# Twelve disjoint views for indirect stores, and a conversion split two issues on, in an attention + expert + feed-forward kernel

## Chip, cores, metric

One core of a Trainium2 chip runs the whole program. The metric is device microseconds of one execution. PE is TensorE, DVE is VectorE, ACT is ScalarE, POOL is GpSimd, SP is SyncE; the last issues most of the loads.

## What is computed

Three layers follow each other on 1536 tokens of width 512, in float32. The first is chunked attention with memory keys. The second sends each token to one of eight experts. The third is a plain feed-forward network. Cut to what matters here:

```python
def _moe_ref(x, w_gate, w1, w2, capacity):
    expert_idx = np.argmax(x @ w_gate, axis=1)
    ...
    h = np.maximum(np.einsum('ecd,edf->ecf', disp, w1), 0.0)
    y = np.einsum('ecf,efd->ecd', h, w2)
    ...
            out[i] = gate_w[i] * y[expert_idx[i], pos[i]]

def _moe2_ref(x, w_in, w_out):
    h = x @ w_in
    g = np.maximum(0.01 * h, h)
    return (g @ w_out)
```

## The kernel before, in words

**Stages.** `prologue` does attention and routing. `experts` then runs expert 0 to 7 one after the other (`expert`, line 746), and `ffn` (line 918) does the last layer. Every float32 product is made of three products of high and low parts, so each weight is first converted into such a pair by ACT and DVE.

**Expert stage.** For each expert, POOL gathers rows of x from HBM by an index table (`gather`, line 634, `nat` tiles, five buffers; line 636 is the indirect DMA). PE transposes them (line 730, in `expert_x`) during the phases of the expert before, then multiplies (line 767, and line 774 for the second product). An expert with over 256 tokens first runs `block` for the rest. The gathers of expert e+2 are issued in phase 3 of expert e (`gathers(e + 2)`). In expert 1, phases 2 and 3 also work out the order in which tokens are sorted by expert (`order`, `sort`): `sort` makes twelve indirect stores of 128 records of three words into the HBM tensor `table` (line 683), and then loads the sorted table back as `srt` (line 685). All of these are in POOL's one queue, in program order, so the gathers of expert 4, issued in expert 2, stand behind the twelve stores and the load.

**Feed-forward stage.** `ffn` makes 48 steps: four quarters of the hidden width (q), three groups of 512 tokens (g), four slices (f). Step n does `gemm3` (line 937, 12 matmuls), `act_h` (ACT lines 943 and 945, DVE lines 944 and 946), then `gemm4` of step n-2 (line 957, 12 matmuls). When a group's four slices are done, `add_up` adds the sums to the output tile, by DVE (line 971) from the second quarter on, and in the last quarter POOL stores each of the twelve tiles of 128 rows to its sorted place by an indirect store (line 973).

**Conversion pieces of the feed-forward weights.** `weights_gen` hands out the 32 pieces of this stage one by one; each `feed(1)` issues one. A piece goes through three parts: at its own issue ACT squares and scales it (lines 128 and 129); one issue later DVE does six operations on it (lines 131 to 139, "the six" below); and `FLIGHT` issues after its own it is split into high (ACT, line 117) and low part (DVE, line 118). Only then it counts as ready. `need` forces an extra `feed` when a product wants a piece that is not ready yet. When no weight slot is free, a feed advances the pieces in flight and issues none. The feeds of the feed-forward stage are given by `FEED_FFN`, nine per quarter for eight pieces:

```python
FEED_FFN = (0, 2, 3, 4, 6, 7, 8, 10, 11)
...
                if rec[1] == 1 or rec[1] == rec[2]:
                    next(rec[0], None)
```

**Order.** Each engine runs its instructions in program order. Waits are put in by a tracker of tile and tensor accesses. It takes two indirect stores into the same tensor for a possible overlap, because the rows are known only at run time.

Of the kernel before, what the change touches and what calls it, by code (L numbers as in the profile page):

```python
# [1 line left out]

# [3 lines left out]

F32 = mybir.dt.float32
# [12 lines left out]
B, H, S, D = 2, 8, 768, 64  # L20
# [7 lines left out]
TPB = S // P  # L28
# [2 lines left out]
RING = 8  # L31
NQ = 4
RAWS, MORE = 5, 3
FLIGHT = 3
SHARE = (0,)
GAP_FEED = 2
WARM = (6, 8, 28)
# [12 lines left out]
class Builder:  # L50
# [470 lines left out]
    def prologue(self):  # L521
        nc = self.nc
        with ExitStack() as ctx:
# [53 lines left out]
            self.wgen = self.weights_gen()  # L577
            self.flight, self.share, self.quarter = FLIGHT, SHARE, 0
            for u in range(NU + 4):
# [99 lines left out]
        dv.tensor_tensor(out=self.rec[:, :, 1], in0=last, in1=keep, op=ALU.mult)  # L679

    def sort(self):
        for t in range(B * TPB):
            self.nc.gpsimd.indirect_dma_start(out=self.table, out_offset=bass.IndirectOffsetOnAxis(
                ap=self.place[:, t:t + 1], axis=0), in_=self.rec[:, t, :], in_offset=None)
        self.nc.gpsimd.dma_start(out=self.srt, in_=self.table.rearrange("(t p) c -> p t c", p=P))

# [231 lines left out]
    def ffn(self):  # L918
        nc = self.nc
        NG, GT, HQ = 3, 512, 4  # L920

        for kind in "AB":
            self.weight_slot((kind, E, 1))
        self.X.append(self.slot(("X", 2), [P, 2, KD, GT], F32R, "x2"))
        wide = self.slot("O", [P, 8, DM], F32, "total")
        rest = [self.mp.tile([P, 2, DM], F32, name="rest", tag="xs", bufs=4) for _ in range(2)]
        total = [wide[:, t, :] for t in range(8)] + [rest[t // 2][:, t % 2, :] for t in range(4)]
        X, nat = self.X, self.rows_of(2, self.ys)
        hps, gs, acc = {}, {}, {}

        def gemm3(s):
            q, g, f = s
            w = self.weight("A", E, q * HQ + f)
            c = slice(f * P, f * P + P)
            hps[s] = self.mps.tile([P, GT], F32, name="h", tag="h", bufs=3)
            for n, (wi, xi, k) in enumerate((wi, xi, k) for wi, xi in ((1, 0), (0, 0), (0, 1)) for k in range(KD)):
                nc.tensor.matmul(hps[s], w[:, wi, k, c], X[g][:, xi, k, :], start=(n == 0), stop=(n == 11))  # L937

        def act_h(s):
            hp = hps.pop(s)  # L940
            t = self.mp.tile([P, GT], F32, name="t", tag="o", bufs=2)
            gt = gs[s] = self.mp.tile([P, 2, GT], F32R, name="gt", tag="hg", bufs=4)
            nc.scalar.copy(out=t, in_=hp)  # L943
            nc.vector.scalar_tensor_tensor(out=t, in0=hp, scalar=0.01, in1=t, op0=ALU.mult, op1=ALU.max)  # L944
            nc.scalar.copy(out=gt[:, 0, :], in_=t)  # L945
            nc.vector.tensor_tensor(out=gt[:, 1, :], in0=t, in1=gt[:, 0, :].bitcast(F32), op=ALU.subtract)  # L946

        def gemm4(ss):
            q, g, f = ss[-1]
            ws = {s: self.weight("B", E, q * HQ + s[2]) for s in ss}  # L950
            gt = {s: gs.pop(s) for s in ss}
            if ss[0][2] == 0:
                acc[g] = [self.mps.tile([P, DM], F32, name="acc", tag="acc", bufs=4) for _ in range(4)]
            for i in range(4):
                for s in ss:
                    for n, (hi, wi) in enumerate(((0, 1), (0, 0), (1, 0))):
                        nc.tensor.matmul(acc[g][i], gt[s][:, hi, i * P:(i + 1) * P], ws[s][:, wi, s[2], :],  # L957
                                         start=(s[2] == 0 and n == 0), stop=(s[2] == HQ - 1 and n == 2))
            if f == HQ - 1:
                add_up(q, g, acc.pop(g))  # L960
                if g == NG - 1:
                    self.retired |= {("A", E, q), ("B", E, q)}

        def add_up(q, g, parts):
            for i in range(4):
                t = g * 4 + i
                sc, o = self.srt[:, t, 2:3].bitcast(F32), total[t]
                if q == 0:
                    nc.scalar.activation(out=o, in_=parts[i], func=AF.Copy, scale=sc)
                else:  # L970
                    nc.vector.scalar_tensor_tensor(out=o, in0=parts[i], scalar=sc, in1=o, op0=ALU.mult, op1=ALU.add)  # L971
                if q == NQ - 1:
                    nc.gpsimd.indirect_dma_start(out=self.out, out_offset=bass.IndirectOffsetOnAxis(  # L973
                        ap=self.srt[:, t, 0:1], axis=0), in_=o, in_offset=None)

        steps = [(q, g, f) for q in range(NQ) for g in range(NG) for f in range(HQ)]
        for n, s in enumerate(steps):
            q, g, f = s
            gemm3(s)
            act_h(s)  # L980
            if 1 < n < len(steps) - 2:
                gemm4([steps[n - 2]])
            if q == 0 and g == 1:
                self.make_x(2, f, nat)
            self.quarter = q + 1
            self.feed(n % len(steps[::NQ]) in FEED_FFN)
        gemm4(steps[-4:-3])
        gemm4(steps[-3:-2])
        gemm4(steps[-2:])
# [61 lines left out]
```

## Time and profile before

| what | value |
|---|---|
| runs before (three) | 617.01, 619.18, 621.42 us; median 619.18 |
| profiled execution | 616.79 us, its span 615.0 us |
| granted TensorE clock, mean | 0.94 |
| packets of the DMA queues | 66377, 84.83 MB |

The span runs from the first to the last instruction that the profiler recorded; the 1.79 us beside it lie outside. Three kinds of views are used below. A timeline row gives start in us, duration in us, engine, line, operation, output<-input, shapes and count; in brackets stands how long the engine sat idle before and what released it. A row of waits gives the sum of idle us, how often, and the longest. A row of windows gives busy time of each engine in a stretch, the granted clock, the share of the DMA engines and GB/s.

### The profile page before, as it was taken

To read this page: it belongs to the slowest core of one execution; us is meant where nothing else is said; L and a number is where in the kernel's file an instruction comes from. 1 tells how busy PE (TensorE), PEld (TensorE's weight loads), DVE (VectorE), ACT (ScalarE), POOL (GpSimd) and SP (SyncE) were. 2 spreads that over 40 slices of the span, in tenths; PEclk is the share of its full clock that TensorE was granted. 3 is DMA by queue.
4 is the path that set the end of the run, shared out by engine and by line. 5 is a ranking of instruction groups with operands and counts; after the bars stand their busy time and mean duration, and the time that the engine had idled before them with its cause. 6 is when DMAs were issued, how large, how long until landed. Compare 5 with 4: busy or idle time off the path is not lost.

```text
span 615.0 us, 9309 instructions
## 1 busy us (share of the span) xinstructions
PE 536.1 (87%) x3313; PEld 433.1 (70%) x3313; DVE 408.6 (66%) x686; ACT 299.9 (49%) x520; POOL 97.8 (16%) x132
## 2 busy tenths in 40 slices
PE   7899948998979594998979999999999999999980
PEld 5566636886967482777967778878877887878870
DVE  5777776864471238882797877868888788854430
ACT  7999646752451348762544455453443444332110
POOL 7422243031211313103102000000000000001121
PEclk7999977998999696899999999999999999999995
DMA  8989949969448529974244212212222110000011
GB/s 190 202 207 193 284 147 352 386 202 305 121 101 227 144 90 341 358 238 155 103 138 137 69 68 70 68 36 68 69 68 70 46 58 0 1 0 35 38 66 68
DMA packets 66377, 84.83 MB, mean 138 GB/s; under 512 B 23168, under 2 KB 39568, under 8 KB 66320
## 3 DMA queue, kind: packets, MB, share of 16 engines
q1 hardware_dynamic: 60016, 66.46, 36.7%
q0 software_dynamic: 5296, 15.77, 8.2%
q10 hardware_dynamic: 1008, 1.84, 0.8%
q8 instruction: 37, 0.61, 0.4%
q14 instruction: 20, 0.16, 0.1%
HBM read 70.66 MB, written 13.39 MB: 137 GB/s over the span
## 4 chain that ended last, share of the span: by engine, by line
DVE 29%; PE 16%; ACT 5%; issue 4%; DMA 2%; ACTq 0%; POOLq 0%
PE acc L957 7%; PE h L937 6%; DVE t L944 4%; DVE gt L946 3%; ACT gt L945 3%; DVE c L138 3%; DVE c L135 3%; DVE c L131 3%; DVE ring L118 3%; DVE c L133 2%; DVE c L137 2%; DVE total L971 2%; DVE c L139 1%; DMA out_dram<-rest,srt 1%; DVE x L697 1%
## 5 line engine op out<-in xcount | busy, mean ns | idle before, releaser
L957 PE MATMUL acc<-ring,gt 128*128 128x512 f32 x576 | 139.1, 391 | 7.7 <-DVE rest L971 2.9
L937 PE MATMUL h<-x,ring 128*128 128x512 f32 x576 | 140.7, 394 | 4.7 <-DVE ring L118 3.7
L957 PEld LDWEIGHTS acc<-ring,gt 128*128 128x128 f32 x576 | 107.5, 188 | 33.4 <-ACT t L943 6.4
L937 PEld LDWEIGHTS h<-x,ring 128*128 128x128 f32 x576 | 108.8, 190 | 28.1 <-DVE ring L118 4.1
L945 ACT CAST gt<-t 128x512 fp32r<-128x512 f32 x48 | 29.8, 621 | 93.7 <-DVE t L944 93.7
L946 DVE TENSOR_TENSOR gt<-t,gt 128x512 fp32r<-128x512 f32 x48 | 33.3, 693 | 33.0 <-ACT gt L945 32.3
L225 DVE TENSOR_TENSOR ring<-raw,ring 128x1024 fp32r<-128x1024 f32 x43 | 50.3, 1221 | 3.1 <-ACT ring L221 2.7
L944 DVE SCALAR_TENSOR_TENSOR t<-h,t 128x512 f32<-128x512 f32 x48 | 32.9, 685 | 29.0 <-ACT t L943 29.0
L767 PE MATMUL h<-xsT,ring 128*128 128x256 f32 x384 | 50.9, 292 | 0.6 <-ACT ring L221 0.6
L943 ACT COPY t<-h 128x512 f32<-128x512 f32 x48 | 28.0, 583 | 46.0 <-PE h L937 45.9
L767 PEld LDWEIGHTS h<-xsT,ring 128*128 128x128 f32 x384 | 49.2, 200 | 1.3 <-ACT ring L221 1.0
L973 POOL DMA_INDIRECT out_dram<-total,srt x8 | 7.8, 975 | 258.9 <-DVE total L971 241.7
L819 DVE SCALAR_TENSOR_TENSOR hs<-h,hs 128x512 fp32r<-128x512 f32 x32 | 21.7, 687 | 41.1 <-ACT hs L818 41.1
L774 PE MATMUL acc<-ring,hs 128*128 128x512 f32 x192 | 45.6, 392 | 0.0
L221 ACT CAST ring<-raw 128x1024 fp32r<-128x1024 f32 x43 | 42.5, 1059 | 0.0
L774 PEld LDWEIGHTS acc<-ring,hs 128*128 128x128 f32 x192 | 35.4, 188 | 6.9
L128 ACT ACTIVATE c<-raw 128x512 f32<-128x512 f32 x32 | 21.9, 684 | 24.8 <-DVE ring L118 24.8
L636 POOL DMA_INDIRECT nat<-xs,tab x24 | 25.3, 1054 | 53.6 <-PE tp L730 36.4
L818 ACT ACTIVATE hs<-h 128x512 fp32r<-128x512 f32 x32 | 18.9, 605 | 26.9 <-PE acc L774 26.9
L867 PE MATMUL h<-ring,xc 128*128 128x512 f32 x72 | 21.6, 452 | 7.9 <-ACT xc L853 7.8
L730 PE MATMUL tp<-ident,nat 128*128 128x128 f32 x64 | 12.9, 329 | 14.5 <-DMA nat<-xs,tab 10.6
L779 PE MATMUL h<-ring,xsT 128*128 128x512 f32 x72 | 22.7, 476 | 3.1 <-DMA nat<-xs,tab 1.5
(183 smaller groups left out, 805.9 us busy)
## 6 DMA issues: line engine op xcount, KB each, us to landing
raw<-in_moe_w_dram SPq DMA_DIRECT2D x43, 512.0 KB
more<-in_moe_w_dram SPq DMA_DIRECT2D x21, 512.0 KB
raw<-in_moe_w_in_dram SPq DMA_DIRECT2D x16, 512.0 KB
raw<-in_moe_w_out_dram SPq DMA_DIRECT2D x16, 512.0 KB
kn<-in_k_dram SPq DMA_DIRECT2D x16, 192.0 KB
qn<-in_q_dram SPq DMA_DIRECT2D x16, 192.0 KB
xs<-x POOLq DMA_DIRECT2D x16, 192.0 KB, 4.7
ys<-o SPq DMA_DIRECT2D x12, 256.0 KB
```

The costliest lines, as they stand in the source:

```text
L221: self.nc.scalar.copy(out=hi, in_=raw)
L225: eng.tensor_tensor(out=lo[:, j:j + n], in0=raw[:, j:j + n], in1=hi[:, j:j + n].bitcast(F32), op=ALU.subtract)
L636: self.nc.gpsimd.indirect_dma_start(out=t, out_offset=None, in_=src, in_offset=bass.IndirectOffsetOnAxis(ap=idx[:, col:col + 1], axis=0))
L767: nc.tensor.matmul(hps[f // 2][:, f % 2 * 256:f % 2 * 256 + 256], w["A", f // 4][:, wi, k, c], xs[xi][:, k, :], start=(n == 0), stop=(n == ...
L774: nc.tensor.matmul(y[j], hs[f // 2][:, hi, c:c + P], w["B", f // 4][:, wi, f % 4, :], start=(f == 0 and n == 0), stop=(f == 7 and n == 2))
L779: nc.tensor.matmul(hps[i], xs[xi][:, k, :P], w["A", i][:, wi, k, :], start=(n == 0), stop=(n == 11))
L937: nc.tensor.matmul(hps[s], w[:, wi, k, c], X[g][:, xi, k, :], start=(n == 0), stop=(n == 11))
L943: nc.scalar.copy(out=t, in_=hp)
L944: nc.vector.scalar_tensor_tensor(out=t, in0=hp, scalar=0.01, in1=t, op0=ALU.mult, op1=ALU.max)
L945: nc.scalar.copy(out=gt[:, 0, :], in_=t)
L946: nc.vector.tensor_tensor(out=gt[:, 1, :], in0=t, in1=gt[:, 0, :].bitcast(F32), op=ALU.subtract)
L957: nc.tensor.matmul(acc[g][i], gt[s][:, hi, i * P:(i + 1) * P], ws[s][:, wi, s[2], :], start=(s[2] == 0 and n == 0), stop=(s[2] == HQ - 1 a ...
```

## The change

`sort` and `ffn` each ask for twelve views of their tensor that the tracker takes as disjoint, and each of the twelve indirect stores goes through its own view. The addresses and the data are the same. `FLIGHT` goes from 3 to 2, so that a piece is split one issue earlier.

```diff
+from concourse.ap import dram_disjoint_views
...
-FLIGHT = 3
+FLIGHT = 2
...
     def sort(self):
+        parts = dram_disjoint_views(self.table, B * TPB)
         for t in range(B * TPB):
-            self.nc.gpsimd.indirect_dma_start(out=self.table, out_offset=bass.IndirectOffsetOnAxis(
+            self.nc.gpsimd.indirect_dma_start(out=parts[t], out_offset=bass.IndirectOffsetOnAxis(
                 ap=self.place[:, t:t + 1], axis=0), in_=self.rec[:, t, :], in_offset=None)
...
+        outs = dram_disjoint_views(self.out, B * TPB)
...
-                    nc.gpsimd.indirect_dma_start(out=self.out, out_offset=bass.IndirectOffsetOnAxis(
+                    nc.gpsimd.indirect_dma_start(out=outs[t], out_offset=bass.IndirectOffsetOnAxis(
```

First place, POOL in experts 1 to 3, where `sort` stands, before. A name DMASW0 to DMASW7 is one of eight counters that POOL's DMAs use in turn and raise when they land; DVE and PE are counters of those engines. Lines L803 and L757 are branches of the experts' code.

```order
L683 DMA table<-rec,place 1536x3 [waits DVE_49,Pool_49]
L683 DMA table<-rec,place 1536x3 [waits DMASW4_49]
L683 DMA table<-rec,place 1536x3 [waits DMASW5_49]
L803 UNCONDITIONAL_BRANCH
L683 DMA table<-rec,place 1536x3 [waits DMASW7_49,DMASW6_49]
L683 DMA table<-rec,place 1536x3 [waits DMASW7_49,DMASW0_49]
L803 UNCONDITIONAL_BRANCH
L683 DMA table<-rec,place 1536x3 [waits DMASW1_49,DMASW0_49]
```

The same place in the changed kernel, whose line numbers are two higher (L685 are the stores, L687 the load, L637 the gathers).

```order
L685 DMA table<-rec,place 1536x3 [waits DVE_49,Pool_49]
L685 DMA table<-rec,place 1536x3 x2
L685 DMA table<-rec,place 1536x3 [waits DMASW7_49]
L685 DMA table<-rec,place 1536x3 [waits DMASW0_49]
L685 DMA table<-rec,place 1536x3 [waits DMASW1_49]
...
L685 DMA table<-rec,place 1536x3 [waits DMASW7_49]
L687 DMA srt<-table 128x12x3 [waits DMASW4_49,DMASW5_49,DMASW3_49,DMASW6_49,DMASW2_49,DMASW7_49,DMASW1_49,DMASW0_49]
L637 DMA nat<-xs,tab 128x512 [waits PE_49]
```

Before, each store waits for the counter of the store just ahead of it. In the changed kernel a store waits only for the counter that it is going to use, that is for the DMA eight places ahead; the load of the sorted table waits for all. The stores of the output change in the same way.

Second place, DVE at the seam of the last expert and the feed-forward stage, before. L697 and L839 end the last expert, L118 is a low part, L131 to L139 are the six, L944 and L946 belong to step 0.

```order
L697 TENSOR_TENSOR x_4914<-tp,x_4914 128x512 x2
L839 COPY o<-acc 128x512
L118 TENSOR_TENSOR ring<-c,ring 128x512
L131 SCALAR_TENSOR_TENSOR c<-c,raw 128x512
L133 TENSOR_SCALAR c<-c 128x512
L135 SCALAR_TENSOR_TENSOR c<-c 128x512
L137 TENSOR_SCALAR c<-c 128x512
L138 TENSOR_TENSOR c<-raw,c 128x512
L139 TENSOR_TENSOR c<-c 128x512
L944 SCALAR_TENSOR_TENSOR t<-h,t 128x512
L946 TENSOR_TENSOR gt<-t,gt 128x512
L118 TENSOR_TENSOR ring<-c,ring 128x512
```

The same place in the changed kernel (L699, L841, L947, L949, L119 and L132 are the same statements).

```order
L699 TENSOR_TENSOR x_4916<-tp,x_4916 128x512 x2
L841 COPY o<-acc 128x512
L947 SCALAR_TENSOR_TENSOR t<-h,t 128x512
L949 TENSOR_TENSOR gt<-t,gt 128x512
L119 TENSOR_TENSOR ring<-c,ring 128x512
L132 SCALAR_TENSOR_TENSOR c<-c,raw 128x512
```

One low part and one round of the six are gone between the copy and step 0: no piece has to be forced there. The low part stands at the beginning of the last expert's phases instead.

Third place, DVE after step 2 of the second quarter, before.

```order
L944 SCALAR_TENSOR_TENSOR t<-h,t 128x512
L946 TENSOR_TENSOR gt<-t,gt 128x512
L118 TENSOR_TENSOR ring<-c,ring 128x512
L944 SCALAR_TENSOR_TENSOR t<-h,t 128x512
L946 TENSOR_TENSOR gt<-t,gt 128x512
L118 TENSOR_TENSOR ring<-c,ring 128x512
L131 SCALAR_TENSOR_TENSOR c<-c,raw 128x512
```

The same place in the changed kernel.

```order
L947 SCALAR_TENSOR_TENSOR t<-h,t 128x512
L949 TENSOR_TENSOR gt<-t,gt 128x512
L119 TENSOR_TENSOR ring<-c,ring 128x512
L132 SCALAR_TENSOR_TENSOR c<-c,raw 128x512
L134 TENSOR_SCALAR c<-c 128x512
L136 SCALAR_TENSOR_TENSOR c<-c 128x512
L138 TENSOR_SCALAR c<-c 128x512
L139 TENSOR_TENSOR c<-raw,c 128x512
L140 TENSOR_TENSOR c<-c 128x512
L947 SCALAR_TENSOR_TENSOR t<-h,t 128x512
```

The six that no longer stand ahead of step 0 stand here, ahead of step 3 of the second quarter; ahead of its step 5 one low part is added as well. The rest of the difference is two low parts that are taken away in the third and fourth quarter and one that is added in the third.

## Rows read from the trace of the kernel before

**Rows 1.** The page: busy us (share of the span) and instructions by engine.
```profile
PE 536.1 (87%) x3313; PEld 433.1 (70%) x3313; DVE 408.6 (66%) x686; ACT 299.9 (49%) x520; POOL 97.8 (16%) x132
```
**Rows 2.** Waits of PE, whole span: us in total, times, longest.
```profile
PE tp L730 <- DMA nat<-xs,tab: 10.6, 4, 7.8
...
PE h L937 <- DVE ring L118: 3.7, 1, 3.7
PE acc L957 <- DVE rest L971: 2.9, 2, 1.5
```
**Rows 3.** Timeline of POOL, 132 to 203: first and last table store, first later gather.
```profile
132.20 1.00 POOL L683 DMA_INDIRECT table<-rec,place  x1 [2.60 <-DVE rec L679]
...
197.47 0.97 POOL L683 DMA_INDIRECT table<-rec,place  x1 [7.50 <-DMA table<-rec,place]
...
202.33 1.01 POOL L636 DMA_INDIRECT nat<-xs,tab  x1 [0.30 <-issue]
```
**Rows 4.** Timeline of PE, 193 to 219, expert 3.
```profile
195.37 3.03 PE L767 MATMUL h<-xsT,ring 128*128 128x256 f32 x24
206.25 0.45 PE L730 MATMUL tp<-ident,nat 128*128 128x128 f32 x1 [7.85 <-DMA nat<-xs,tab]
...
216.42 2.91 PE L774 MATMUL acc<-ring,hs 128*128 128x512 f32 x12
```
**Rows 5.** Timeline of PE, 153 to 166, the same code in expert 2.
```profile
154.47 3.04 PE L767 MATMUL h<-xsT,ring 128*128 128x256 f32 x24
...
163.53 2.68 PE L774 MATMUL acc<-ring,hs 128*128 128x512 f32 x11
```
**Rows 6.** Timeline of all engines, 316 to 329, seam of experts and feed-forward stage.
```profile
317.36 0.94 PE L937 MATMUL h<-x,ring 128*128 128x512 f32 x3
...
319.50 0.68 DVE L839 COPY o<-acc 128x512 f32<-128x512 f32 x1
320.57 0.62 ACT L117 CAST ring<-c 128x512 fp32r<-128x512 f32 x1 [1.86 <-DVE o L839]
321.23 0.69 DVE L118 TENSOR_TENSOR ring<-c,ring 128x512 fp32r<-128x512 f32 x1 [1.05 <-ACT ring L117]
...
321.97 7.37 PE L937 MATMUL h<-x,ring 128*128 128x512 f32 x24 [3.67 <-DVE ring L118]
...
326.43 0.69 DVE L944 SCALAR_TENSOR_TENSOR t<-h,t 128x512 f32<-128x512 f32 x1 [0.81 <-ACT t L943]
```
**Rows 7.** Timeline of DVE, 404 to 480, second quarter and start of the third.
```profile
408.18 0.69 DVE L118 TENSOR_TENSOR ring<-c,ring 128x512 fp32r<-128x512 f32 x1
410.49 0.69 DVE L944 SCALAR_TENSOR_TENSOR t<-h,t 128x512 f32<-128x512 f32 x1 [1.63 <-ACT t L943]
...
413.08 0.69 DVE L131 SCALAR_TENSOR_TENSOR c<-c,raw 128x512 f32<-128x512 f32 x1
...
416.78 0.68 DVE L944 SCALAR_TENSOR_TENSOR t<-h,t 128x512 f32<-128x512 f32 x1
...
478.72 0.69 DVE L944 SCALAR_TENSOR_TENSOR t<-h,t 128x512 f32<-128x512 f32 x1 [2.02 <-ACT t L943]
```
**Rows 8.** Timeline of DVE, 591 to 600: the last sum of the output.
```profile
597.94 0.75 DVE L971 SCALAR_TENSOR_TENSOR rest<-acc,srt,rest 128x512 f32<-128x512 f32 x1 [0.61 <-PE acc L957]
```
**Rows 9.** Chain that ended last, 590 to 616: start, us, what.
```profile
594.62 0.39 issue
...
598.51 2.77 DMA out_dram<-rest,srt
```
**Rows 10.** Timeline of POOL, 593 to 615: the last output store.
```profile
610.77 0.97 POOL L973 DMA_INDIRECT out_dram<-rest,srt  x1 [2.54 <-DMA out_dram<-rest,srt]
```
**Rows 11.** The line of the table stores, all twelve: issue to landing.
```profile
DMA to landing us min/median/max: 2.9/4.6/6.4
```
**Rows 12.** Windows, 142 to 150: busy by engine, clock, DMA share, GB/s.
```profile
142.00:150.00 8.00, 8.00 (x34) 6.03 (x33) 3.19 (x6) 1.35 (x3) 2.03 (x2) 0.81 1.04 355
```
**Rows 13.** Timeline of ACT, 157 to 163: next weight conversions after the stores' start.
```profile
159.32 2.97 ACT L221 CAST ring<-raw 128x1024 fp32r<-128x1024 f32 x3
```

## Prediction

> **What bounds the kernel now.** I read four views. The page says that PE is busy 87% of the span [rows 1], so the 13% in which it is not are what a change of waits can win, and a few stages where PE follows another engine. The view of PE's waits names them: the largest wait of the whole program is for gathered rows [rows 2], and a smaller one is for the low part of a feed-forward weight. The timeline of POOL shows why the gather is late: the twelve table stores begin at 132.20 and the last begins at 197.47, 65 us for work that takes POOL about 1 us each, and the first gather behind them starts at 202.33 [rows 3]. The chain that ended last shows the third place: after the last sum of the output the span holds nothing but output stores, one behind the landing of the other [rows 8 to 10].
>
> In the feed-forward stage the reader is to see who leads. In the second quarter DVE goes on from 410.49 to 478.72 without idling for a first operation of a step (the row at 478.72 is the next with such a wait) [rows 7], apart from a short wait inside each step. So there a DVE instruction more is time lost, as far as no idle time takes it up.
>
> **Term 1, the table stores.** Twelve stores keep their number and their size; what goes is eleven waits for a landing. POOL then issues one about each 1.0 + 0.3 us (durations and idle time of [rows 3]), twelve in 16 us, to about 148. The load of the sorted table waits for all, which by the longest landing of 6.4 us [rows 11] is about 154, and the gathers behind it start near 156, each when its row buffer is free, instead of at 202.33. The added wait on a counter eight places back costs POOL at most one landing. Behind it stand only the load and these gathers, and their reader, PE, asks at 195.37 + 3.03 = 198.40 [rows 4], 40 us later. So the cover is wide.
>
> What PE gains is read against the same code one expert earlier, where the rows were there. From the first units (line 767) to the first second product (line 774) expert 3 takes 216.42 - 195.37 = 21.05 us [rows 4], expert 2 takes 163.53 - 154.47 = 9.06 us [rows 5]. The difference is 12.0 us. Of this 7.85 us are the idle time in the row at 206.25 alone; the rest is a second wait and slower matmuls behind it. Bounds: 7.9 us if only that idle time goes, 12.5 us if the block ahead also gets quieter. I take 12.0, since the row of expert 2 is the same code. What is late next at 198.40? The transposed rows of expert 4 are then followed by units whose weights are converted, as in expert 2, so nothing near.
>
> **Term 2, the seam at the feed-forward stage.** Before, step 0 of the stage needs a fourth piece that isn't split, so a feed is forced: DVE does the low part at 321.23 and the six behind it, and PE idles 3.67 us until 321.97 [rows 6]. Split one issue earlier, this piece is ready and no feed is forced. Then DVE goes from the copy at 319.50 straight to step 0. One low part (0.6 us from start to start, 321.23 against the next at 321.84 in the same view) now stands in the last expert, whose DVE has no gap here, so the copy comes at 320.1. ACT is free for step 0 at 320.57 + 0.6 = 321.2, PE's first product is done by then (twelve matmuls of 512 columns stream as many as the 24 of 256 that took 3.04 us [rows 5]: 317.36 + 0.6 + 3.04 = 321.0), ACT copies for 0.6 us, and DVE starts step 0 at 321.85 instead of 326.43 [rows 6]: 4.6 us earlier. In the first quarter PE follows DVE, so I count it fully. Bounds: 2.5 us (PE's wait of 3.67 less 0.6 for the low part in the last expert, and as much again for unknowns) and 5.3 us.
>
> **Term 3, the piece comes back.** The six that were forced ahead of step 0 now stand ahead of step 3 of the second quarter. They take 416.78 - 413.08 = 3.70 us [rows 7]. DVE has idle time there: the low part at 408.18 would let go at 408.8, and the next step starts at 410.49 [rows 7], 1.7 us. So 2.0 us come through; with a low part of 0.6 us ahead of step 5 it is 2.6 us. From there DVE is the leader until the sums of the quarter's last group are added up, and PE waits for those sums (the row on line 971) [rows 2], so the third quarter starts 2.6 us later. Bounds: 0 if the slack of 2.02 us at 478.72 [rows 7] and PE's own take it up, 4.3 if no idle time takes up any of it. The three other low parts that move lie beside idle time.
>
> **Term 4, the output stores.** The last sum ends at 597.94 + 0.75 = 598.69 [rows 8]. A store starts some 0.39 us after its release [rows 9], so the last could start at 599.1, since the three ahead of it wait only for sums that came before. From the last store's start to the end of the span the trace has 615.0 - 610.77 = 4.2 us [rows 10], which stays. So the span's end moves from 615.0 to 603.3: 11.7 us. Bounds: 9.0 if overlapping stores land later than the 2.77 us of one alone [rows 9], 12.2 at best.
>
> **The sum.** 12.0 + 4.6 - 2.6 + 11.7 = 25.7 us earlier. Against the profiled execution this is 616.79 - 25.7 = 591.1; that one lay 2.4 us below the median of three. The median is what a new measurement comes near, so I forecast 619.18 - 25.7 = 593.5 us. A measurement of this kernel can tell about 1% from no change, some 6 us.
>
> **A rule that speaks against it.** A table record is 12 bytes. The row says that such a store lands in 2.9 to 6.4 us [rows 11], against 2.77 us for an output store with rows of 2 KB [rows 9], so small records cost little alone. The Trainium skill (DMA: Bandwidth & Descriptors, Specifications) says that below 512 B a DMA engine reads, changes and writes back. By that rule twelve stores at once would load the engines more than their bytes say; no row shows them at once. It would be the slower rival below, and the fastest landing of 2.9 us does not bear it out.
>
> **Rivals.**
>
> *The output queue does one store after the other anyway.* Then the tail stays as it was, and only terms 1 to 3 are left: 14.0 us, 605.2 us. For it: all stores go through POOL's one queue, and no output store was in flight with another before. Against it: gathers on the same queue start without waiting for each other, as the one at 202.33, which starts 0.3 us after the load ahead of it [rows 3]. The Trainium skill (DMA: Bandwidth & Descriptors, Anatomy of one DMA — SWDGE (gpsimd) path) puts most of such a DMA's fixed time into the receipt of its last write, which is time that another could use; by that rule the stores overlap and the tail shrinks as in term 4.
>
> *PE's wait for the rows gives way to another.* If the next thing (weights, or the buffers of expert 3's outputs) holds PE almost as long at 198.40, term 1 shrinks to about 2 us: 619.18 - 15.7 = 603.5. For it: DMA is nearly full while weights load (share 1.04) [rows 12]. Against it: expert 2 shows no such wait [rows 5].
>
> *The split costs more than it gives.* If DVE leads in the second quarter and the first quarter's gain is lost, terms 2 and 3 are +4.3 instead of -2.0: 599.8 us.
>
> *Slower than before: the burst of records blocks the weights.* Twelve stores within 16 us share the DMA engines with the next expert's weights, which ACT converts at 159.32 [rows 13]. If each held the engines alone for its whole 6.4 us [rows 11], twelve would hold them 77 us, until 209, and the conversions would be 50 us late: 593.5 + 50 = 643 us. It decides against the change once a store holds the engines for more than (159.32 - 132.20 + 25.7) / 12 = 4.4 us. Against it: from 142 to 150, while the stores were landing at their slowest, the engines moved 355 GB/s [rows 12].
>
> **How the numbers follow.** Forecast 0.72, tail unchanged 0.08, another wait in place of the gather 0.10, split costs more 0.07, slower 0.03. Only the last is not faster by over 1%, and a mix of two bad cases can land near no change: faster 0.95, within 1% 0.02, slower 0.03. The range: at the low end the profiled execution's level with good bounds, 616.79 - 12.5 - 5.3 + 2.0 - 12.2 = 588.8, so 588; at the high end the median with poor bounds, 619.18 - 7.9 - 2.5 + 2.6 - 9.0 = 602.4, and to take in the rival at 603.5, 604.
>
> **What would show it.** Term 1: the table stores' line starts all twelve within about 20 us of 132, and PE's wait for gathered rows falls from 10.6 to near 3 us. Term 2: PE's wait of 3.7 us for the low part is gone and step 0 follows the copy. Term 3: DVE does not idle ahead of step 3 of the second quarter, and PE waits longer there for sums of line 971 (974 in the changed kernel). Term 4: the last four output stores start about 1.4 us apart, and the span ends some 4.6 us after the last sum. The prediction is wrong if a wait of over 5 us for weights appears between 150 and 215, if stores still start 3.5 us apart, or if the span is over 602.

## The result and the profile after

The changed kernel takes 597.88 us (median of 4 runs, 595.99 to 599.83) against 619.25 us of the kernel before on the same chip (median of 4). The ratio is 0.9655, 95% interval 0.9601 to 0.9710: 21.4 us less. The forecast was 593.5 us with a range of 588 to 604. The profiled execution of the changed kernel took 596.13 us, its span is 594.4 us, and the mean granted clock is 0.958 (0.94 before).

PE does the same work in less time. The page's engines, as in [rows 1]:

```profile
PE 530.9 (89%) x3313; PEld 429.0 (72%) x3313; DVE 408.6 (69%) x686; ACT 298.8 (50%) x520; POOL 99.4 (17%) x132
```

The counts are those of before. PE's busy share goes from 87% to 89%, because idle time goes and little of its work. POOL is busy 1.6 us longer; where is shown below.

The waits of PE over the whole span, as in [rows 2] (us in total, times, longest):

```profile
PE acc L960 <- DVE total L974: 4.3, 3, 1.9
...
PE acc L960 <- DVE ring L119: 3.0, 2, 2.6
PE acc L960 <- DVE rest L974: 2.9, 2, 1.5
PE tp L732 <- DMA nat<-xs,tab: 2.9, 2, 1.9
```

The wait for gathered rows is down from 10.6 to 2.9 us, and the 3.7 us ahead of line 940 (937 before) are gone. The waits for sums (`total`, line 974) and for a low part in the second product (line 960) are now the larger ones, where DVE leads. In the kernel before the same two were:

```profile
PE acc L957 <- DVE total L971: 1.9, 2, 1.0
PE acc L957 <- DVE ring L118: 1.8, 3, 0.6
```

A second profile of the changed kernel (it runs once more below) has 2.8 us for `total`, so the wait is longer in both, but not by a fixed amount.

**The table stores.** POOL, as in [rows 3]:

```profile
133.35 0.99 POOL L685 DMA_INDIRECT table<-rec,place  x1 [2.60 <-DVE rec L680]
134.65 1.85 POOL L685 DMA_INDIRECT table<-rec,place  x1 [0.30 <-issue]
136.80 1.95 POOL L685 DMA_INDIRECT table<-rec,place  x1 [0.30 <-issue]
...
151.49 0.97 POOL L685 DMA_INDIRECT table<-rec,place  x1 [0.55 <-DMA table<-rec,place]
161.74 1.08 POOL L687 DMA_DIRECT2D srt<-table  x1 [9.29 <-DMA table<-rec,place]
163.12 1.01 POOL L637 DMA_INDIRECT nat<-xs,tab  x1 [0.30 <-PE h L769]
```

All twelve start within 18.1 us instead of 65.3. The line of these stores now lands later, though, than in [rows 11]:

```profile
DMA to landing us min/median/max: 3.0/9.9/12.2
```

So the load waits 9.29 us and the first gather behind it starts at 163.12, not near 156. It hurts nobody. PE, expert 3, as in [rows 4]:

```profile
196.94 3.04 PE L769 MATMUL h<-xsT,ring 128*128 128x256 f32 x24
199.81 0.60 PE L732 MATMUL tp<-ident,nat 128*128 128x128 f32 x4
200.17 5.99 PE L769 MATMUL h<-xsT,ring 128*128 128x256 f32 x48
206.00 2.91 PE L776 MATMUL acc<-ring,hs 128*128 128x512 f32 x12
```

PE asks for the rows at 199.81 and they are there. From the first units to the first second product it takes 206.00 - 196.94 = 9.06 us, to the hundredth what expert 2 takes in [rows 5].

**The seam.** All engines, as in [rows 6]:

```profile
309.21 2.00 ACTq L844 DMA_DIRECT2D ys<-o  x2
310.18 0.68 DVE L841 COPY o<-acc 128x512 f32<-128x512 f32 x1
313.28 0.59 ACT L946 COPY t<-h 128x512 f32<-128x512 f32 x1 [4.10 <-DMA ys<-o]
313.90 0.69 DVE L947 SCALAR_TENSOR_TENSOR t<-h,t 128x512 f32<-128x512 f32 x1 [3.05 <-ACT t L946]
```

No low part and no six stand between the copy (line 841) and step 0 any more. But step 0 doesn't follow the copy: ACT's copy of PE's product into `t` waits 4.10 us, and what it waits for is a store of the last expert's results.

**The second quarter.** DVE, as in [rows 7]:

```profile
393.78 0.69 DVE L947 SCALAR_TENSOR_TENSOR t<-h,t 128x512 f32<-128x512 f32 x1 [2.10 <-ACT t L946]
...
400.07 0.68 DVE L947 SCALAR_TENSOR_TENSOR t<-h,t 128x512 f32<-128x512 f32 x1
```

Step 3 starts without idle time ahead of it, where before there were 1.63 us (the row at 410.49 in [rows 7]).

**The tail.** All engines from 583 on, as in [rows 8, 10]:

```profile
585.07 0.97 POOL L976 DMA_INDIRECT out_dram<-rest,srt  x1 [7.51 <-DVE rest L974]
585.40 0.75 DVE L974 SCALAR_TENSOR_TENSOR rest<-acc,srt,rest 128x512 f32<-128x512 f32 x1 [0.61 <-PE acc L960]
586.43 0.97 POOL L976 DMA_INDIRECT out_dram<-rest,srt  x1 [0.39 <-DVE rest L974]
586.76 0.75 DVE L974 SCALAR_TENSOR_TENSOR rest<-acc,srt,rest 128x512 f32<-128x512 f32 x1 [0.61 <-PE acc L960]
588.12 0.75 DVE L974 SCALAR_TENSOR_TENSOR rest<-acc,srt,rest 128x512 f32<-128x512 f32 x1 [0.61 <-PE acc L960]
588.82 0.98 POOL L976 DMA_INDIRECT out_dram<-rest,srt  x1 [1.42 <-issue]
590.11 0.97 POOL L976 DMA_INDIRECT out_dram<-rest,srt  x1 [0.30 <-issue]
```

The stores overlap: the one at 590.11 starts 1.29 us behind the one at 588.82, and a store alone takes 2.77 us to land [rows 9]. The last sum ends at 588.87, the last store starts 1.24 us later instead of 12.08. The third store is late: its sum ended at 586.76 + 0.75 = 587.51, it starts at 588.82, and the trace names no releaser for its 1.42 us of idle time.

**Where the 20.7 us between the two spans went.** Each row is the length of a stretch in the profiled execution, between the starts of the same instructions (the last but one starts at the end of the last sum).

| stretch | before | after | difference |
|---|---|---|---|
| start to first table store | 132.20 | 133.35 | +1.15 |
| to the first units of expert 2 | 22.27 | 23.29 | +1.02 |
| to the first units of expert 3 | 40.90 | 40.30 | -0.60 |
| to the first second product of expert 3 (term 1) | 21.05 | 9.06 | -11.99 |
| to the first line 819 (821) of expert 7 | 79.26 | 79.58 | +0.32 |
| to step 0 of the feed-forward stage (term 2) | 30.75 | 28.32 | -2.43 |
| first quarter | 69.30 | 69.43 | +0.13 |
| second quarter (term 3) | 67.41 | 69.99 | +2.58 |
| third quarter | 68.23 | 68.21 | -0.02 |
| fourth quarter to the end of the last sum | 67.32 | 67.34 | +0.02 |
| last sum to last output store (term 4) | 12.08 | 1.24 | -10.84 |
| last store to the end | 4.25 | 4.25 | 0.00 |

### The profile page after: what moved, and what is told of

Read it like the earlier page. It is cut to its first block, busy times and chain, and to the rows that moved or that the text cites. A ratio compares the mean times of both kernels' runs of the same rounds, so it can differ in the third digit from the quotient of the medians.

```text
span 594.4 us, 9319 instructions
## 1 busy us (share of the span) xinstructions
PE 530.9 (89%) x3313; PEld 429.0 (72%) x3313; DVE 408.6 (69%) x686; ACT 298.8 (50%) x520; POOL 99.4 (17%) x132
## 4 chain that ended last, share of the span: by engine, by line
DVE 30%; PE 10%; issue 8%; ACT 6%; POOL 2%; DMA 1%; ACTq 0%; POOLq 0%
DVE t L947 4%; DVE gt L949 4%; ACT gt L948 4%; DVE c L139 3%; DVE c L136 3%; DVE c L132 3%; PE acc L960 3%; DVE ring L119 3%; PE h L940 2%; DVE c L134 2%; DVE c L138 2%; DVE total L974 2%; POOL out_dram L976 2%; DVE c L140 1%; PE h L869 1%
## 5 line engine op out<-in xcount | busy, mean ns | idle before, releaser
L960 PE MATMUL acc<-ring,gt 128*128 128x512 f32 x576 | 140.8, 395 | 11.2 <-DVE total L974 4.3
L940 PE MATMUL h<-x,ring 128*128 128x512 f32 x576 | 138.8, 391 | 1.1 <-ACT x L698 1.1
L949 DVE TENSOR_TENSOR gt<-t,gt 128x512 fp32r<-128x512 f32 x48 | 33.3, 694 | 33.0 <-ACT gt L948 33.0
L947 DVE SCALAR_TENSOR_TENSOR t<-h,t 128x512 f32<-128x512 f32 x48 | 32.9, 685 | 30.2 <-ACT t L946 30.2
L946 ACT COPY t<-h 128x512 f32<-128x512 f32 x48 | 28.0, 584 | 50.1 <-PE h L940 45.9
L769 PE MATMUL h<-xsT,ring 128*128 128x256 f32 x384 | 48.8, 285 | 0.6 <-DVE ring L226 0.6
L769 PEld LDWEIGHTS h<-xsT,ring 128*128 128x128 f32 x384 | 47.1, 191 | 1.3 <-ACT ring L222 1.0
L637 POOL DMA_INDIRECT nat<-xs,tab x24 | 24.5, 1020 | 82.6 <-PE tp L732 49.4
L226 DVE TENSOR_TENSOR ring<-more,ring 128x1024 fp32r<-128x1024 f32 x21 | 24.6, 1221 | 0.6 <-ACT ring L222 0.5
L869 PEld LDWEIGHTS h<-ring,xc 128*128 128x128 f32 x72 | 15.0, 217 | 13.1 <-ACT xc L855 8.5
```

Source lines behind the costliest of these rows:

```text
L226: eng.tensor_tensor(out=lo[:, j:j + n], in0=raw[:, j:j + n], in1=hi[:, j:j + n].bitcast(F32), op=ALU.subtract)
L637: self.nc.gpsimd.indirect_dma_start(out=t, out_offset=None, in_=src, in_offset=bass.IndirectOffsetOnAxis(ap=idx[:, col:col + 1], axis=0))
L769: nc.tensor.matmul(hps[f // 2][:, f % 2 * 256:f % 2 * 256 + 256], w["A", f // 4][:, wi, k, c], xs[xi][:, k, :], start=(n == 0), stop=(n == ...
L869: nc.tensor.matmul(hp[i], xc[:, xi, k, :], w[:, wi, k, :], start=(n == 0), stop=(n == 11))
```

## The experiments

**The change taken apart.** My theory was that the two sets of views give nearly all of the gain, each at its own place, and that the earlier split gives little. The rivals were that the split matters, and that the two sets of views win the same time. Four kernels ran on one chip, on which the kernel before took 614.78 us. The times that I expected for them were reckoned from the 619 us of the first comparison, so what is to be compared is the ratio.

Both sets of views with the split where it was, an edit to the changed kernel:

```diff
-FLIGHT = 2
+FLIGHT = 3
```

> Both sets of views, split three issues on as before. Theory (the four terms): the views carry everything, the split nets +0.2 us (-2.4 at the seam, +2.6 in the second quarter), so this runs as the changed kernel, 597 to 599 us; PE's wait of about 3.7 us for the low part at the seam is back, and the second quarter is 2.6 us shorter. Rival (the split itself helps by 4 us or more): 602 us or more. Rival (the split costs): 595 us or less.

Measured: 595.46 us, ratio 0.9679 (0.9646 to 0.9711). This is the whole gain of the change within the intervals. PE's wait that the split took away is back:

```profile
PE h L940 <- DVE ring L119: 3.7, 1, 3.7
```

The second quarter takes 67.41 us as before, and the seam takes 29.93 us. So the earlier split gives 1.6 us at the seam against this run (2.4 us against the kernel before), and takes 2.6 us in the second quarter.

The split alone, an edit to the kernel before:

```diff
-FLIGHT = 3
+FLIGHT = 2
```

> No views, split two issues on. Theory: -2.4 us at the seam and +2.6 us in the second quarter cancel, 619 us, no difference that can be measured. Rival (the split helps): 615 us or less. Rival (it costs): 623 us or more.

Measured: 617.19 us, ratio 1.0046 (1.0020 to 1.0071), which is 2.8 us slower (1.2 to 4.4). I had expected no difference that can be measured, and that was wrong. The stretch of the seam is 28.57 us, the second quarter 69.99 us: -2.2 and +2.6, close to the changed kernel's -2.4 and +2.6, which make +0.4. The 2.8 us of the ratio are more than that, and what the rest is stays open. The span of its profile, 610.1 us, was shorter than before's 615.0 for another reason, the wait for gathered rows in the view of PE's waits:

```profile
PE tp L730 <- DMA nat<-xs,tab: 6.7, 4, 3.2
```

In that execution the twelfth store started at 192.29 and not at 197.47, and PE's stretch in expert 3 was 15.37 us and not 21.05. With the same code the wait that term 1 removes has another size in another execution.

The table views alone (the changed kernel without the output views, split three on):

```diff
-FLIGHT = 2
+FLIGHT = 3
...
-        outs = dram_disjoint_views(self.out, B * TPB)
...
-                    nc.gpsimd.indirect_dma_start(out=outs[t], out_offset=bass.IndirectOffsetOnAxis(
+                    nc.gpsimd.indirect_dma_start(out=self.out, out_offset=bass.IndirectOffsetOnAxis(
```

> Views for the table stores alone, split three issues on. Theory: the wait for gathered rows and the slow matmuls behind it go, 12.0 us: 607 us; the output stores still run one behind the landing of the other. Rival (the wait only moves and comes back later in the experts): 613 us or more.

Measured: 606.07 us, ratio 0.9856 (0.9817 to 0.9895), which is 8.9 us of 614.78 (6.5 to 11.3). The stretch of expert 3 is 9.06 us. The tail is the old one, on POOL:

```profile
590.61 0.97 POOL L975 DMA_INDIRECT out_dram<-rest,srt  x1 [2.56 <-DMA out_dram<-rest,srt]
595.83 0.98 POOL L975 DMA_INDIRECT out_dram<-rest,srt  x1 [4.24 <-issue]
599.35 0.97 POOL L975 DMA_INDIRECT out_dram<-rest,srt  x1 [2.54 <-DMA out_dram<-rest,srt]
```

The last but one is the late store here too, by 1.7 us more than its neighbours' 2.5.

The output views alone (the changed kernel without the table views, split three on):

```diff
-FLIGHT = 2
+FLIGHT = 3
...
-        parts = dram_disjoint_views(self.table, B * TPB)
...
-            self.nc.gpsimd.indirect_dma_start(out=parts[t], out_offset=bass.IndirectOffsetOnAxis(
+            self.nc.gpsimd.indirect_dma_start(out=self.table, out_offset=bass.IndirectOffsetOnAxis(
```

> Views for the output stores alone, split three issues on. Theory: the tail shrinks by about 11 us: 608 us; the table stores take 65 us as before and PE waits some 8 us for gathered rows. Rival (stores of one queue go one after the other whatever the waits): 616 us or more.

Measured: 603.10 us, ratio 0.9826 (0.9764 to 0.9889), which is 10.7 us of 614.78 (6.8 to 14.5). The last store starts 1.23 us after the last sum. PE waits for rows in expert 3 as before, a little less long:

```profile
204.76 0.45 PE L731 MATMUL tp<-ident,nat 128*128 128x128 f32 x1 [6.29 <-DMA nat<-xs,tab]
206.16 0.90 PE L731 MATMUL tp<-ident,nat 128*128 128x128 f32 x3 [0.95 <-DMA nat<-xs,tab]
```

8.9 + 10.7 = 19.6 us; both together gave 0.0321 of 614.78, 19.7 us. Within their intervals the two gains add up, and the profiles show them at different places.

**How large the wait is without the change.** The kernel before once more, later, for one profile. The split alone and the output views alone count here too, since their `sort` is that of before.

> The kernel before, one more profile. Theory (the wait for gathered rows depends on how late the serial table stores land in that execution): the stretch from expert 3's first units to its first second product again differs, between 15 and 21 us, and goes with the start of the twelfth store. Rival (it is always 21 us, and the runs without views that showed less differ by their own edits): 21 us again.

Measured: 620.38 us in the one execution. PE in expert 3:

```profile
197.33 3.03 PE L767 MATMUL h<-xsT,ring 128*128 128x256 f32 x24
210.33 0.45 PE L730 MATMUL tp<-ident,nat 128*128 128x128 f32 x1 [9.97 <-DMA nat<-xs,tab]
...
219.46 2.91 PE L774 MATMUL acc<-ring,hs 128*128 128x512 f32 x12
```

The stretch is 22.13 us, longer than in any other and a little outside the 15 to 21 us that I had expected; the twelfth store came later than in any other as well. The four executions without the table views:

| kernel | twelfth store | first second product of expert 3 | difference | stretch | over 9.06 |
|---|---|---|---|---|---|
| before | 197.47 | 216.42 | 18.95 | 21.05 | 12.0 |
| before again | 201.97 | 219.46 | 17.49 | 22.13 | 13.1 |
| output views alone | 196.32 | 214.04 | 17.72 | 18.60 | 9.5 |
| split alone | 192.29 | 210.92 | 18.63 | 15.37 | 6.3 |

PE goes on 17.5 to 19.0 us after the twelfth store starts, whatever the stretch. So the added wait goes with how long the twelve landings in a row happened to be: 6.3 to 13.1 us, mean 10.2. With the table views the stretch was 9.06 or 9.07 us in all ten profiles.

**What holds step 0 at the seam.** The theory: the copy into `t` for step 0 goes into the buffers of tag "o", the two that the last expert's results use, so it has to wait until the store of these results (line 844) has landed. The rival: the copy waits for PE's product or for ACT itself, and the releaser is wrongly named. If the theory holds, other buffers for the last expert's results bring the step forward by 2 us with the early split, and by nothing with the late one, where the forced feed takes longer than the landing. Both on one chip, with 616.41 us for the kernel before:

```diff
-        o = [self.npool.tile([P, DM], F32, name="o", tag="o", bufs=2) for _ in range(2)]
+        o = [self.gpool.tile([P, DM], F32, name="nat", tag="nat", bufs=5) if e == E - 1 else
+             self.npool.tile([P, DM], F32, name="o", tag="o", bufs=2) for _ in range(2)]
```

> The changed kernel, but the two result tiles of the last expert lie in the buffers of the gathered rows, so that step 0's tile t no longer takes a buffer from which a store is still leaving. Theory: the changed kernel loses 2.0 us at the seam because ACT's copy for step 0 waits for that store's landing; here it starts 2 us earlier, right behind the first product, 596 us. Rival (something else holds step 0): no change, 598 us, and the copy still starts 2 us behind the product.

Measured: 594.02 us, ratio 0.9661 (0.9623 to 0.9699). The stretch to step 0 is 26.35 us (28.32 to 28.57 without the edit). The seam:

```profile
308.18 2.02 ACTq L845 DMA_DIRECT2D ys<-nat  x2
309.16 0.68 DVE L842 COPY nat<-acc 128x512 f32<-128x512 f32 x1
310.30 0.59 ACT L947 COPY t<-h 128x512 f32<-128x512 f32 x1 [2.15 <-DVE nat L842]
310.92 0.69 DVE L948 SCALAR_TENSOR_TENSOR t<-h,t 128x512 f32<-128x512 f32 x1 [1.08 <-ACT t L947]
```

ACT goes on 1.14 us after DVE's copy starts, not 3.10. It doesn't follow PE's first product at once, as I had expected: ACT's own queue first issues the two stores, the second of them behind DVE's copy, until 308.18 + 2.02 = 310.20. The 2 us are shown by the profile alone, for the ratio is no lower than the changed kernel's 0.9655.

The same edit with the split three on:

```diff
-FLIGHT = 2
+FLIGHT = 3
```

> As the run before, with the split three issues on. Theory: there PE's wait for the low part holds step 0, and the store has landed by then, so nothing is won: the same as views alone, 597 to 599 us. Rival: 2 us less than views alone.

Measured: 595.25 us, ratio 0.9677 (0.9641 to 0.9712), stretch 30.10 us, against 29.93 us of the views alone with the same split: nothing, as the theory says. With the shared buffers the stretch is 29.93 to 31.15 us in the five profiles with the late split and 28.32 to 28.58 us in the five with the early one. So the split alone gives some 2.2 us, the buffers give theirs only on top of it, and together they give 30.75 - 26.35 = 4.4 us.

**Giving the second quarter its time back.** Nine feeds per quarter for eight pieces let one round of the six and one low part stand ahead of a quarter's first step, where DVE leads. The last feed of a quarter is taken away:

```diff
-FEED_FFN = (0, 2, 3, 4, 6, 7, 8, 10, 11)
+FEED_FFN = (0, 2, 3, 4, 6, 7, 8, 10)
```

> The changed kernel with eight feeds per quarter instead of nine: the feed behind the last step of each quarter is dropped, so one conversion piece per quarter boundary comes later and the last two fall into the fourth quarter, where DVE idles. Theory (in quarters two and three DVE leads and PE waits for the sums): the stalls of some 9.7 us between the second quarter and the third step of the fourth shrink by 3 to 4 us: 594 us. Rival (PE's pace or ACT sets the end there): no change, 598 us. Rival (pieces come too late): 600 us or more.

Measured: 591.72 us, ratio 0.9599 (0.9569 to 0.9629). DVE around the start of the second quarter:

```profile
378.07 0.68 DVE L947 SCALAR_TENSOR_TENSOR t<-h,t 128x512 f32<-128x512 f32 x1
379.44 0.69 DVE L949 TENSOR_TENSOR gt<-t,gt 128x512 fp32r<-128x512 f32 x1 [0.69 <-ACT gt L948]
381.50 0.69 DVE L947 SCALAR_TENSOR_TENSOR t<-h,t 128x512 f32<-128x512 f32 x1 [1.36 <-ACT t L946]
```

The steps at 378.07 and 381.50 lie 3.4 us apart. In the changed kernel the same two lie 6.3 us apart:

```profile
377.04 0.68 DVE L947 SCALAR_TENSOR_TENSOR t<-h,t 128x512 f32<-128x512 f32 x1
...
383.33 0.68 DVE L947 SCALAR_TENSOR_TENSOR t<-h,t 128x512 f32<-128x512 f32 x1
```

By the starts of DVE's steps, the first quarter takes 66.51 us (69.43), the second 67.98 (69.99), the third 68.01 (68.21). The fourth gives 0.8 us back: up to its step 3 it takes 17.20 us (15.59), from there to the end of the last sum 50.91 (51.76). In sum that is -4.4 us. PE gets it later than DVE: at the start of the second quarter it doesn't wait in either kernel. What shrinks are its waits for sums, all of them behind that start. In the changed kernel they were 4.3 + 2.9 + 0.9 = 8.1 us (lines 974 and 972; 6.7 us in its second profile), and with eight feeds this one row is left:

```profile
PE acc L960 <- DVE total L974: 4.2, 4, 1.5
```

Both edits together:

> Own buffers for the last expert's results and eight feeds per quarter together. Theory: the two gains add, 592 us. Rival (what is won at the seam is lost behind it): as eight feeds alone, 594 us.

Measured: 592.29 us, ratio 0.9634 (0.9588 to 0.9681). The profile has both effects (26.34 us to step 0, first quarter 66.43 us) and its span is the shortest of all profiles, 589.2 us, but the median does not lie below that of the eight feeds alone.

To see how these compare, three kernels ran once more, on a chip that has the same number on record as that of the first four kernels. The kernel before took 619.51 us there this time, not 614.78, so times are compared only within one group of runs. The changed kernel as it is:

> The changed kernel once more, beside the two that may beat it. Expected: about 3.4% under the kernel before; the first second product of expert 3 comes 9.06 us after its first units, as in every run with table views.

Measured: 597.45 us, ratio 0.9656 (0.9603 to 0.9709). Eight feeds:

> The changed kernel with eight feeds per quarter, on the same chip as the changed kernel. Theory: 3 to 4 us (0.5 to 0.6%) under the changed kernel, won between the second quarter and the third step of the fourth. Rival: no difference.

Measured: 592.58 us, ratio 0.9542 (0.9498 to 0.9585). Eight feeds and own buffers:

> Eight feeds and own buffers for the last expert's results, on the same chip. Theory: 2 us under eight feeds alone, 5 to 6 us under the changed kernel. Rival (the seam's gain is lost again): as eight feeds alone.

Measured: 591.59 us, ratio 0.9540 (0.9499 to 0.9581). Eight feeds beat the changed kernel by 4.9 us on the same chip, and the two intervals do not touch. With the buffers it is 1 us less there and was 0.6 us more in the comparison before; their 2 us are in every profile at their place, but on top of the eight feeds the medians don't show them.

## Why the prediction was right

**Term 1 had the right mechanism and a size from one execution.** The stores start together, the wait is gone, and nothing else is late at that place. The step that failed in size was "I take 12.0, since the row of expert 2 is the same code". The target, 9.06 us, was exact; the starting point, 21.05 us, was one draw. The table views alone gave 8.9 us (6.5 to 11.3), and the four profiles without them have 6.3 to 13.1. The lower bound of 7.9 us, too, came from that one execution. Part of the gap to 10.2 us may be a price that I had put at nothing: from the first store to the first units of expert 2 the kernels without table views took 22.22 to 22.42 us, those with them 21.69 to 24.45. Up to the first units of expert 3 it is 63.2 us in the mean of four without and 64.2 us in the mean of ten with them. In the changed kernel the block ahead of these units (of expert 2's tokens beyond 256) ran slower, at a granted clock that was lower than in [rows 12]:

```profile
142.00:150.00 8.00, 8.00 (x25) 6.30 (x26) 3.21 (x5) 0.63 (x3) 6.17 (x7) 0.63 0.96 251
```

That this price comes from the stores isn't shown: in the ten profiles with the views the clock there is between 0.63 and 1.00, and in the four without them 0.79 to 0.81.

**The landing was misjudged, under wide cover.** The "longest landing of 6.4 us [rows 11]" came from stores that were alone; the twelve that start within 18.1 us land after 9.9 us (median), so the load came at 161.74 instead of 154. PE asks at 199.81, and the gather's start at 163.12 leaves 36 us.

**Term 2 failed at one step, "ACT is free for step 0 at 320.57 + 0.6 = 321.2, PE's first product is done by then (...), ACT copies for 0.6 us".** It left out the buffer that the copy is written to. ACT and PE were ready, and the copy waited for a store's landing: the gain was 2.4 us in this pair of profiles and 2.2 us between the means of five each, instead of 4.6, and under my lower bound of 2.5. With own buffers it is 4.4 us. So the rest of the working stands; the buffers were shared in the kernel before too, where the forced feed took longer than the landing.

**Term 3 was right:** the second quarter took 2.58 us longer, forecast 2.6. DVE leads there, and counting its instructions less the idle time ahead of the next step gave the price to 0.1 us.

**Term 4 was right but for one store:** 10.84 of 11.7 us. The step "A store starts some 0.39 us after its release [rows 9], so the last could start at 599.1" took every store for that. The first two of the last four start 0.28 us after the end of their sums, the third 1.31 us after, and the fourth comes 1.29 us behind it, so the last store starts 1.23 or 1.24 us after the last sum in every profile with the output views. In the profile of before the third is the store with 4.24 us of idle time ahead of it. Why is open. So the four starts are 1.36, 2.39 and 1.29 us apart where I expected about 1.4, and the span ends 5.49 us after the last sum where I expected 4.6. My upper bound of 12.2 us was more than the 12.08 us that there were to win.

**The sum.** 10.2 + 2.4 - 2.6 + 10.8 = 20.8 us from the profiles, 21.4 us measured (interval 18.0 to 24.7), 25.7 forecast, which lies above that interval. Three of the four terms were read high, all from the ideal end, term 2 by nearly half. The range was wide enough for that. It took term 3 at 2.0 and 2.6 us, though its own bounds were 0 and 4.3; with these it would have been 586.8 to 604.1.

**The rivals.** *The output queue does one store after the other*: refuted by the starts 1.3 us apart in the tail. *PE's wait gives way to another*: refuted by 9.06 us. *The split costs more than it gives*: by the profiles terms 2 and 3 together are +0.2 us, where I had -2.0 and this rival +4.3; the split alone measured +2.8 us (1.2 to 4.4). So my sign was wrong, and the truth lies between the two.

*The burst blocks the weights*: the burst loads the DMA engines, but no conversion of weights waited for it. In the windows of 142 to 150 us the engines moved 355 to 366 GB/s in the four profiles without table views, and 218 to 273 GB/s in nine of the ten with them, at a busy share of 0.90 to 1.00 against 1.02 to 1.05 (the tenth, whose stores begin 4 us later, has 310 GB/s at 1.13). Worked out from the two rows of the windows, (355 - 251) GB/s for 8 us are 0.8 MB that other transfers lack, some 2.3 us at 355 GB/s; the rival needed 50 us. The next weight conversion came 27.1 to 27.3 us after the first table store without table views, and 27.5 to 31.0 us after it with them. In none of the fourteen profiles does a conversion have over 0.3 us of idle time ahead of it between 130 and 215. What comes late is a copy by ACT in the block of expert 2, ahead of these conversions; first the row of before, then the changed kernel's:

```profile
154.72 0.37 ACT L897 COPY o<-acc 128x256 f32<-128x256 f32 x1 [3.98 <-PE acc L885]
161.21 0.37 ACT L899 COPY o<-acc 128x256 f32<-128x256 f32 x1 [8.30 <-DMA ys<-o]
```

It waits for a store of the results of expert 1 to land, since it is written to the buffers of tag "o" as well; it is the trap of the seam, at another place. In this profile PE isn't held by it: from the first units of expert 2 to those of expert 3 it takes 40.30 us (40.90 before). In all ten with table views that is 40.27 to 41.91 us, without them 40.89 to 41.03. The Trainium skill (DMA: Bandwidth & Descriptors, Specifications) says that transfers under 512 B are read, changed and written back. Engines as busy with fewer bytes agree with that, though no run here varied the size of a record.

## What to carry to other kernels

Indirect stores into one tensor each wait for the landing of the one before, unless the program says that they are disjoint; look for a row of equal idle times on the issuing queue, and price them by who asks for the data at the end. Price a wait for DMA landings from several executions: here it was 6.3 to 13.1 us with the same code. When a stall is taken away, list what else the next instruction waits for, the buffer it writes to included; and where an engine leads, as DVE in the second quarter, count its instructions and ask whether one feed less does.

## What was not expected of the hardware

Four of the twelve table stores kept POOL busy 1.85 to 1.97 us instead of 0.97, all while DVE ran these operations:

```profile
134.41 5.77 DVE L226 TENSOR_TENSOR ring<-raw,ring 128x1024 fp32r<-128x1024 f32 x5 [0.24 <-ACT ring L222]
140.10 3.48 DVE L226 TENSOR_TENSOR ring<-more,ring 128x1024 fp32r<-128x1024 f32 x3
```

Those are 134.41 to 143.58, and the stores that start outside took 0.96 to 0.99 us. The Trainium skill (SBUF — State Buffer, SBUF: two separate sides) says that a DVE operation with two SBUF inputs and a GpSimd operation that reads SBUF take a pair of ports from each other for the whole instruction. The trace agrees: one of the five takes 5.77 / 5 = 1.15 us, so the first ends at 135.56, and the store at 134.65 ends at 136.50, 0.94 us later. The twelve stores keep POOL busy 15.5 us in all, 12.7 before: 2.8 us more, which is more than the 1.6 us by which the page's sum grew, as the gathers of rows took 0.8 us less. None of it is on PE's path.
